# Token groups that follow the batches: one pooled attention and MLP kernel, regrouped

## The chip, the cores and the metric

The kernel runs on one core of one Trainium2 chip. The metric is device time in microseconds of one launch. The kernel before was run five times; one execution was also profiled, and every line of a profile below is from such an execution.

## What is computed

There are 8 batches of 8 heads with 576 queries of 64 numbers. Keys and values are averaged over runs of 8 positions, so that 72 of them stand against 576 queries. The attention output, with the heads side by side, gives 4608 tokens of 512 numbers, which pass a two-layer MLP with the activation h - tanh(h).

```python
def _attn_ref(q, k, v):
    k_p = k.reshape(B, H, Sp, pool, D).mean(axis=3)
    v_p = v.reshape(B, H, Sp, pool, D).mean(axis=3)
    scores = scale * np.matmul(q, k_p.transpose(0, 1, 3, 2))
    scores = scores - np.max(scores, axis=-1, keepdims=True)
    attn = np.exp(scores)
    attn = attn / (np.sum(attn, axis=-1, keepdims=True) + 1e-09)
    return np.matmul(attn, v_p).astype(np.float32)

def _moe_ref(x, w_in, w_out):
    h = x @ w_in
    g = h - np.tanh(h)
    return (g @ w_out).astype(np.float32)
```

## The kernel before

The MLP works on nine groups of 512 tokens (TG = 512, NG = 9). A batch has 576 tokens (S), so group g takes tokens 512g to 512g+511 across batch borders. Inside a batch the first 512 queries (QA) are held as position p*4 + j, so that a block of 128 tokens is one j; the last 64 (QT) are a tail block.

The order of all instructions is written out by hand, and each engine works through its own in that order. TensorE is PE in the profile, VectorE DVE, ScalarE ACT, GpSimd POOL; SP issues most of the DMAs.

**Groups 0 and 1.** Batch 0 is loaded, pooled and transposed on TensorE. Group 0's first layer runs tile by tile (`mlp_h`, L512), its second layer in 16 steps u (`mlp_o`, L540), with the preparation of batch 1 between them: `k_transpose`, `q_pe_transpose` (L217), `scores_wide`, `av` and `x_pe_transpose` (L475). The PSUM banks for all of these rotate over three.

**Groups 1 to 8.** A group has two stages.

- The h stage: 16 tiles of the first layer, four matmuls each (`h_mms`, L558), mostly in pairs. For a pair, ScalarE takes tanh (L570), VectorE subtracts (L571), and further VectorE operations form sums (P, Q). In this stage batch nb = g + 1 has its queries cast on ScalarE (`q_cast_part`, L192 and L197), and SP issues a transpose of k (L334) and five of q (L205). Then SP issues the loads of k, v and q of batch g + 2 (nine DMAs, about 3.4 MB), in one stream with the transposes. GpSimd finishes pooling, then issues the stores of group g - 1 (`store_tile`, L635) and places k (L302).
- The products: seven products of the second layer (a scheme that saves one of eight), each in two halves of eight matmul pairs, so u = 0 to 13 (L614), collected in two PSUM banks and combined by ScalarE and VectorE (`after_product`, L654 to L674). Between them stand the scores of batch nb (u = 0 to 4, each tile of 576 columns as two of 288, L351 and L370) and its attention blocks (u = 6, 7, 8, 9 and 11: `av_both`, matmuls L398, reciprocal L433, multiply L434). SP transposes each block of x into xT (L463) by DMA.

The activations for the MLP are in `xT`, a ring over three groups' tokens. Which blocks of a batch are transposed at once, and which wait for the next group's stage, follows from the group's border:

```python
            if b * S + blk * 128 < (b + 1) * TG:
                x_dma_transpose(b, blk, x_sb)
            else:
                late.append((b, blk, x_sb))
```

A block that crosses the end of the ring takes two transposes, and a tile of output that crosses a batch border takes two stores (`out_segments`).

**The end.** Group 8 has no attention beside it. Its last product is done token tile by token tile (L1025), each followed by a copy and its stores; the stores of the third and fourth output part go out from SP, GpSimd and ScalarE (L631, L1028). Line L1056 holds the program's closing waits.

Of the kernel before, what the change touches and what calls it, by code (L numbers as in the profile page):

```python
# [19 lines left out]
NHP = H // 2  # L20
# [3 lines left out]
T = B * S  # L24
NFB = DM // 128
# [9 lines left out]
RING = 3 * TG  # L35
# [7 lines left out]
def kernel(  # L43
# [54 lines left out]
    xT = const.tile([128, NFB, RING], BF16, name="xT")  # L98
# [100 lines left out]
    def q_dma_transpose(b, j0=0, j1=R + 1):  # L199
        if j0 == 0:  # L200
            qTs[b] = work.tile([128, NHP, S], BF16, name="qT", tag="qT")
        qT = qTs[b]
        for j in range(j0, j1):
            rows = 128 if j < R else QT
            nc.sync.dma_start_transpose(  # L205
                out=qT[:, :, j * 128 : j * 128 + rows],
                in_=q_bf[:rows, j, :, :].rearrange("p h d -> p (h d)"),
            )

    def q_pe_transpose(b, hps, eng=None):  # L210
        if b not in qTs:
            qTs[b] = work.tile([128, NHP, S], BF16, name="qT", tag="qT")
        qT = qTs[b]
        for hp in hps:
# [9 lines left out]
            evac(qT[:, hp, 0:QA], ps[:, :], eng)  # L224

    def q_pe_tail(b):
        ps = ps_any([128, NHP, QT], FP32, "qt_ps")
        for hp in range(NHP):
            nc.tensor.matmul(
                ps[:, hp, :],  # L230
                lhsT=q_bf[:, R, 2 * hp : 2 * hp + 2, :].rearrange("p h d -> p (h d)"),
                rhs=ident[:, 0:QT],
                start=True,
                stop=True,
            )
        evac(qTs[b][:, :, QA:S], ps[:, :, :])
# [109 lines left out]
    def score_mms(b, t, dst, c0, c1, pairs=range(NM)):  # L346
        for m in pairs if t == NM else (t,):
# [6 lines left out]
                rhs=qTs[b][:, m, c0:c1],  # L354
                start=True,
                stop=True,
            )

    def scores(b, t):
        if t == 0:  # L360
            E_tiles[b] = work.tile([128, NT, S], BF16, name="E", tag="E", bufs=1)
        E = E_tiles[b]
        hs = S // 2
        pss = []
        for half in range(2):
            ps = ps_b1([128, hs], FP32, "s_ps")
            score_mms(b, t, ps[:, :], half * hs, (half + 1) * hs)
            pss.append(ps)
        for half, ps in enumerate(pss):
            nc.scalar.activation(  # L370
                out=E[:, t, half * hs : (half + 1) * hs], in_=ps[:, :], func=ACT.Exp, scale=SCALE
            )

    def scores_wide(b, ts):
# [3 lines left out]
        for t in ts:  # L378
            ps = ps_any([128, QA], FP32, "s_ps")
            score_mms(b, t, ps[:, :], 0, QA)  # L380
            nc.scalar.activation(out=E[:, t, 0:QA], in_=ps[:, :], func=ACT.Exp, scale=SCALE)

    def scores_tail(b):
        ps = ps_any([128, NT, QT], FP32, "s_ps")
        for t in range(NT):
            score_mms(b, t, ps[:, t, :], QA, S)
# [36 lines left out]
    def new_x():  # L423
        return work.tile([128, 2, 4, D], BF16, name="x_sb", tag="x_sb", bufs=5)

# [15 lines left out]
    def av(b, blk, alloc, by_dma):  # L441
        x_sb = new_x()
        if by_dma:
# [4 lines left out]
        if by_dma:  # L448
            if b * S + blk * 128 < (b + 1) * TG:
                x_dma_transpose(b, blk, x_sb)  # L450
            else:
                late.append((b, blk, x_sb))
        return x_sb

    late = []

    def x_dma_transpose(b, blk, x_sb):
        p0 = 0 if blk < 4 else 64
        pos = (b * S + blk * 128) % RING
        p1 = min(128, p0 + RING - pos)  # L460
        for r0, r1, c in ((p0, p1, pos), (p1, 128, 0)):
            if r1 > r0:
                nc.sync.dma_start_transpose(  # L463
                    out=xT[:, :, c : c + r1 - r0],
                    in_=x_sb[r0:r1, :, :, :].rearrange("p a h d -> p (a h d)"),
                )

    def x_pe_transpose(b, blk, x_sb, fbs=(0, 4)):
        p0 = 0 if blk < 4 else 64
        pos = b * S + blk * 128  # L470
        f0, f1 = fbs
        xf = x_sb.rearrange("p a h d -> p (a h d)")
        ps = ps_any([128, f1 - f0, 128], FP32, "xT_ps")
        for fb in range(f0, f1):
            nc.tensor.matmul(  # L475
                ps[:, fb - f0, p0:128],
                lhsT=xf[:, fb * 128 : (fb + 1) * 128],
                rhs=ident[:, p0:128],
# [3 lines left out]
        nc.scalar.copy(out=xT[:, f0:f1, pos : pos + 128 - p0], in_=ps[:, :, p0:128])  # L482

    def out_segments(c0, nrows):
        segs = []
        r = 0
        while r < nrows:
            c = c0 + r
            bb = c // S
            i = c % S  # L490
            if i < QA:
                j = i // 128
                p0 = i % 128
                ln = min(128 - p0, nrows - r, QA - i)
                dst = out[bb * S : bb * S + QA, :].rearrange("(p j) m -> p j m", j=R)[
                    p0 : p0 + ln, j, :
                ]
            else:
                ln = min(S - i, nrows - r)
                dst = out[bb * S + i : bb * S + i + ln, :]  # L500
            segs.append((r, r + ln, dst))
            r += ln
        return segs
# [3 lines left out]
    def mlp_h_mms(g, i, f0, f1, pool=None):  # L507
        tok0 = g * TG
        if f0 == 0:
            h_tiles[i] = ps_h.tile([128, TG]) if pool is None else pool  # L510
        for fb in range(f0, f1):
# [3 lines left out]
                rhs=xT[:, fb, tok0 : tok0 + TG],  # L515
# [18 lines left out]
    def mlp_o(g, tb, i0, i1, gts, pool=None):  # L534
# [12 lines left out]
        if i1 == NHID:  # L547
# [4 lines left out]
            for r0, r1, dst in out_segments(g * TG + tb * 128, 128):  # L552
                nc.sync.dma_start(out=dst, in_=o_sb[r0:r1, :])

    def h_mms(g, i, dst):
        c0 = (g * TG) % RING
        for fb in range(NFB):
# [3 lines left out]
                rhs=xT[:, fb, c0 : c0 + TG],  # L561
# [66 lines left out]
    def store(g, th, engs, c0, c1):  # L628
        for tt in range(2):
# [431 lines left out]
```

## Time and profile before

| | us |
|---|---|
| median of 5 runs | 295.13 |
| lowest and highest | 293.11 and 297.32 |
| the profiled execution | 295.13 |
| its span, first to last instruction | 293.4 |
| TensorE busy | 279.9 |
| VectorE busy | 223.6 |
| ScalarE busy | 153.3 |
| GpSimd busy | 135.8 |
| h matmuls L558, 496 recorded | 112.6 |

DMA issues from the page:

| transfer | count | us from issue to landing, median |
|---|---|---|
| xT<-x_sb, transpose, SP | 32 | 3.4 |
| qT<-q_bf, transpose, SP | 30 | 2.5 |
| kT<-kd, transpose, SP | 6 | 3.1 |
| out<-O, 256 KB, GpSimd | 12 | 3.4 |
| out<-O, 128 KB, GpSimd | 32 | 3.6 |
| out<-O, 64 KB, SP | 12 | 2.2 |

How to read it: times are from the start of the span. A busy TensorE is not TensorE at its peak, since the ends of matmuls are modelled. "A <- B" in a list of waits means that A sat idle until B was done, with the total in us, the number of times and the longest. The time of a run is 1.7 us longer than the span.

### The profile page before, as it was taken

What the parts mean: (1) busy time and instruction counts of PE and PEld (TensorE: products, weight loads), DVE (VectorE), ACT (ScalarE), POOL (GpSimd) and SP (SyncE); (2) the same over time, 40 slices, a digit from 0 to 9 for tenths busy, and PEclk for the clock granted to TensorE, in tenths of its full rate; (3) what the DMA queues carried; (4) which work ended last, traced back from release to release, by engine and by line L of the source; (5) the groups of instructions that cost most, each with busy time, mean ns of one, the idle gap of its engine ahead of it and who ended that gap; (6) DMA issues with size and microseconds to landing.
All of it is one profiled execution on the core that took longest, in us unless ns stands there. A gap on an engine that the chain in (4) does not pass through costs nothing.

```text
span 293.4 us, 5359 instructions
## 1 busy us (share of the span) xinstructions
PE 279.9 (95%) x2017; PEld 179.0 (61%) x2036; DVE 223.6 (76%) x348; ACT 153.3 (52%) x242; POOL 135.8 (46%) x160
## 2 busy tenths in 40 slices
PE   7999989999999996999999999999999999999992
PEld 2454455446874685448954895489548944874681
DVE  5658665799977995389959967996799849927971
ACT  4737586586347732566176618661867046226510
POOL 8600818980299339900797089608960040030001
PEclk9999999999999999799999999999999999999998
DMA  7999999948835999599937996799581260021023
GB/s 253 229 213 282 308 210 315 303 90 303 193 78 109 287 303 115 123 243 324 84 76 186 351 188 87 196 343 182 78 205 28 56 171 2 0 77 69 0 57 89
DMA packets 65098, 49.91 MB, mean 170 GB/s; under 512 B 40336, under 2 KB 54032, under 8 KB 65072
## 3 DMA queue, kind: packets, MB, share of 16 engines
q1 hardware_dynamic: 55184, 35.53, 52.0%
q0 software_dynamic: 7312, 12.19, 18.3%
q10 hardware_dynamic: 2576, 1.84, 2.2%
q8 instruction: 16, 0.26, 0.4%
q14 instruction: 10, 0.08, 0.1%
HBM read 36.70 MB, written 9.44 MB: 157 GB/s over the span
## 4 chain that ended last, share of the span: by engine, by line
PE 84%; DVE 6%; DMA 3%; ACT 3%; issue 1%; SPq 0%; ACTq 0%; DVEq 0%
PE PS L558 34%; PE PS L614 33%; PE PS L540 5%; PE PS L398 4%; PE PS L351 4%; PE PS L512 2%; DMA k_raw<-in_k_dram 2%; DVE Gt L571 2%; DVE Gt L525 1%; DMA xT<-x_sb 1%; ACT q_bf L192 1%; DVE P L579 1%; ACT TS L570 0%; PE PS L475 0%; PE PS L800 0%
## 5 line engine op out<-in xcount | busy, mean ns | idle before, releaser
L558 PE MATMUL PS<-xT,w1b 128*128 128x512 bf16 x496 | 112.6, 383 | 3.1 <-DMA xT<-x_sb 2.3
L571 DVE TENSOR_TENSOR Gt<-PS,TS 128x1024 bf16<-128x1024 f32 x56 | 68.4, 1221 | 29.8 <-ACT TS L570 29.7
L558 PEld LDWEIGHTS <-w1b 128*128 128x128 f16 x512 | 50.3, 98 | 63.0 <-issue 5.0
L570 ACT ACTIVATE TS<-PS 128x1024 f32<-128x1024 f32 x56 | 57.4, 1025 | 34.4 <-PE PS L558 29.1
L248 POOL TENSOR_TENSOR k_raw<-k_raw 128x512 f32<-128x512 f32 (+2 forms) x13 | 21.1, 1639 | 75.9 <-DVE rden L433 46.2
L635 POOL DMA_DIRECT2D out_dram<-O x44 | 23.8, 547 | 39.9 <-DVE O L673 22.3
L614 PE MATMUL PS<-w2s,Dg 128*128 128x256 f16 x256 | 30.2, 273 | 0.0
L614 PEld LDWEIGHTS <-Gt 128*128 128x128 bf16 x256 | 24.4, 98 | 5.7 <-DVE Gt L576 0.5
L614 PEld LDWEIGHTS <-P 128*128 128x128 bf16 x256 | 24.6, 98 | 4.7 <-issue 1.4
L614 PEld LDWEIGHTS <-Dg 128*128 128x128 bf16 x256 | 24.5, 98 | 2.6
L434 DVE TENSOR_TENSOR x_sb<-PS,rden 128x512 bf16<-128x512 f32 x30 | 20.7, 691 | 6.8 <-DMA xT<-x_sb 5.9
L370 ACT ACTIVATE E<-PS 128x288 bf16<-128x288 f32 x60 | 21.4, 409 | 8.0 <-PE PS L351 7.6
L579 DVE TENSOR_TENSOR P<-Gt 128x1024 bf16<-128x1024 bf16 x32 | 22.2, 693 | 0.6
L398 PE MATMUL PS<-VB,E 128*128 128x130 bf16 x240 | 20.2, 220 | 0.1
L670 ACT COPY m<-PS 128x512 f32<-128x512 f32 x8 | 4.7, 586 | 29.5 <-PE PS L614 29.5
L269 POOL TENSOR_TENSOR v_raw<-v_raw 128x512 f32<-128x512 f32 (+1 forms) x12 | 20.1, 1694 | 0.0
L589 DVE TENSOR_TENSOR Dg<-Gt 128x1024 bf16<-128x1024 bf16 x32 | 19.9, 683 | 0.0
L398 PEld LDWEIGHTS <-E 128*128 128x128 bf16 x240 | 16.8, 98 | 1.9 <-issue 0.4
L351 PE MATMUL PS<-qT,KB 128*128 128x288 bf16 (+5 forms) x128 | 17.0, 289 | 0.2
L614 PE MATMUL PS<-w2s,Gt 128*128 128x256 f16 x128 | 16.7, 273 | 0.3 <-DVE Gt L576 0.2
L1021 ACT COPY O<-PS 128x512 f32<-128x512 f32 x7 | 4.1, 586 | 24.5 <-PE PS L614 24.5
L614 PE MATMUL PS<-w2s,P 128*128 128x256 f16 x128 | 16.3, 273 | 0.0
(112 smaller groups left out, 387.5 us busy)
## 6 DMA issues: line engine op xcount, KB each, us to landing
k_raw<-in_k_dram SPq DMA_DIRECT2D x7, 1024.0 KB, 8.7
q_raw<-in_q_dram SPq DMA_DIRECT2D x7, 1024.0 KB, 11.8
v_raw<-in_v_dram SPq DMA_DIRECT2D x7, 1024.0 KB, 11.9
out_dram<-O POOLq DMA_DIRECT2D x32, 128.0 KB, 3.6
out_dram<-O POOLq DMA_DIRECT2D x12, 256.0 KB, 3.4
w1b<-in_moe_w_in_dram POOLq DMA_DIRECT2D x4, 512.0 KB, 13.9
w2b<-in_moe_w_out_dram POOLq DMA_DIRECT2D x4, 512.0 KB, 17.1
out_dram<-O SPq DMA_DIRECT2D x4, 256.0 KB, 4.5
```

Source lines behind the costliest of these rows:

```text
L248: first = eng.tensor_tensor(out=r[:, ta:tb, 0:4, :], in0=r[:, ta:tb, 0:4, :], in1=r[:, ta:tb, 4:8, :], op=ALU.add)
L269: eng.tensor_tensor(out=r[:, ta:tb, 0:4, :], in0=r[:, ta:tb, 0:4, :], in1=r[:, ta:tb, 4:8, :], op=ALU.add)
L351: nc.tensor.matmul(dst[p : p + w], lhsT=KB[b % 2][:, o : o + w], rhs=qTs[b][:, m, c0:c1], start=True, stop=True,)
L370: nc.scalar.activation(out=E[:, t, half * hs : (half + 1) * hs], in_=ps[:, :], func=ACT.Exp, scale=SCALE)
L398: nc.tensor.matmul(ps[:, 2 * n : 2 * n + 2, :].rearrange("p h d -> p (h d)") if n < 2 else ps.rearrange("p (a s) d -> p a s d", s=2)[:, :, ...
L434: nc.vector.tensor_tensor(out=x_sb[:, :, :, :], in0=ps[:, :, :, 0:D], in1=rden[:, :, :, :].to_broadcast([128, 2, 4, D]), op=ALU.mult,)
L558: nc.tensor.matmul(dst, lhsT=w1b[:, fb, i * 128 : (i + 1) * 128], rhs=xT[:, fb, c0 : c0 + TG], start=(fb == 0), stop=(fb == NFB - 1),)
L570: nc.scalar.activation(out=t2, in_=PS[:, b0 : b0 + 2, :], func=ACT.Tanh)
L571: nc.vector.tensor_sub(out=Gt[:, p, :, :], in0=PS[:, b0 : b0 + 2, :], in1=t2)
L579: nc.vector.tensor_tensor(out=P[:, a:b, :], in0=Gt[:, a:b, 0, :], in1=Gt[:, a:b, 1, :], op=ALU.add)
L614: nc.tensor.matmul(part(g, bk, tt), lhsT=lhs(k, slice(tt * 128, (tt + 1) * 128)), rhs=rhs[:, k, :], start=(first and k == 0 and (tt == 0 o ...
L635: nc.gpsimd.dma_start(out=dst, in_=O[r0:r1, tb, :])
```

## The change

Groups 0 to 7 now are the first 512 queries of batches 0 to 7, and group 8 is the eight tails of 64. So `xT` becomes two tiles used in turn, each [128, 4 blocks, 4 feature blocks, 128], and a third, `xT_last`, for group 8. A group's right-hand operand for L558 comes from four pieces of 128 columns. All four blocks of batch g + 1 are due at the start of group g + 1.

The blocks of x are kept in pairs, and one DMA transposes a pair, 128 x 1024; the tail block has its own. Queries do the same: two transposes of 1024 columns and one of the tail, for five of 512. In groups 1 to 6, scores are formed as 512 columns per tile (`scores_wide`) at u = 0 to 4 and the tails of all tiles at u = 5 (`scores_tail`); the attention blocks come at u = 5, 6, 7, 8 and 10. Batch 0's tail goes to xT_last by DMA, not through TensorE; the tail of batch 1 is transposed at the start of group 1. One q transpose of batch 1 on TensorE moves from u = 3 to u = 4, and the next two one step on.

A group's stores on GpSimd are two of 512 KB. In group 8 each store is two, by partition halves (the two batches of a token tile), on SP or on SP and ScalarE, none on GpSimd; both last copies are VectorE's.

```diff
-    xT = const.tile([128, NFB, RING], BF16, name="xT")
+    xT = [const.tile([128, 4, NFB, 128], BF16, name=f"xT{i}") for i in range(2)]
+    xT_last = const.tile([128, 4, NFB, 128], BF16, name="xT_last")
...
+    def q_dma_transpose(b, n):
+        qT, qt = q_tiles(b)
+        if n < 2:
             nc.sync.dma_start_transpose(
-                out=qT[:, :, j * 128 : j * 128 + rows],
-                in_=q_bf[:rows, j, :, :].rearrange("p h d -> p (h d)"),
+                out=qT[:, 2 * n : 2 * n + 2, :, :].rearrange("p j h c -> p (j h) c"),
+                in_=q_bf[:, 2 * n : 2 * n + 2, :, :].rearrange("p j h d -> p (j h d)"),
+            )
...
+    def x_dma_transpose(b, n):
+        if n < 2:
+            nc.sync.dma_start_transpose(
+                out=xT[b % 2][:, 2 * n : 2 * n + 2, :, :].rearrange("p k f c -> p (k f) c"),
+                in_=x_pairs.pop((b, n)).rearrange("p k a h d -> p (k a h d)"),
+            )
+        else:
+            c = (b % 2) * QT
+            nc.sync.dma_start_transpose(
+                out=xT_last[:, b // 2, :, c : c + QT],
+                in_=x_pairs.pop((b, 2))[128 - QT : 128].rearrange("p a h d -> p (a h d)"),
+            )
...
     def h_mms(g, i, dst):
-        c0 = (g * TG) % RING
+        x = xT[g % 2] if g < NB else xT_last
...
-                rhs=xT[:, fb, c0 : c0 + TG],
+                rhs=x[:, :, fb, :],
...
+    def store(g, t0, t1, eng, c0=0, c1=DM):
+        if g < NB:
+            eng.dma_start(out=out_part(g, t0, t1, c0, c1), in_=O[:, t0:t1, c0:c1])
+        else:
+            for k, dst in enumerate(out_part(g, t0, t1, c0, c1)):
+                eng[k].dma_start(out=dst, in_=O[k * QT : (k + 1) * QT, t0:t1, c0:c1])
...
         if i == 11:
-            x4 = av(0, 4, ps_any, False)
-        if i == 13:
-            x_pe_transpose(0, 4, x4)
+            av(0, 4, ps_any, False)
+            x_dma_transpose(0, 2)
...
-            q_pe_transpose(1, (0, 1), "act")
+            q_pe_transpose(1, (0,), "act")
         if u == 4:
-            q_pe_transpose(1, (2,), "act")
+            q_pe_transpose(1, (1,), "act")
...
-        if u == 5:
-            q_pe_transpose(1, (3,), "act")
+        if u in (5, 6):
+            q_pe_transpose(1, (u - 3,), "act")
...
+            if g == 1 and p == 0:
+                x_dma_transpose(1, 2)
             if g > 1 and p == 0:
-                for tb in (2, 3, 0, 1):
-                    store_tile(g - 1, tb)
+                store(g - 1, 2, 4, nc.gpsimd)
+                store(g - 1, 0, 2, nc.gpsimd)
...
-                q_dma_transpose(nb, 2 * c, min(2 * c + 2, R + 1))
+                q_dma_transpose(nb, c)
...
-        while late:
-            x_dma_transpose(*late.pop(0))
...
-                    scores(nb, u)
+                    scores_wide(nb, (u,))
                 if u == NT:
-                    ps_a.n += 2
-                if u in (6, 7, 8, 9, 11):
-                    av(nb, (6, 7, 8, 9, 11).index(u), ps_b1, True)
+                    scores_tail(nb)
+                if u in (5, 6, 7, 8, 10):
+                    blk = (5, 6, 7, 8, 10).index(u)
+                    av(nb, blk, ps_b1, True)
+                    if blk in (1, 3, 4):
+                        x_dma_transpose(nb, blk // 2)
...
-    store(NG - 1, 1, (nc.sync, nc.gpsimd), HD, DM)
+    ends = (nc.sync, nc.scalar)
+    store(NG - 1, 2, 4, ends, HD, DM)
     bk, lhs, rhs = products[6]
-    for tt, eng in ((0, nc.scalar.copy), (1, nc.vector.tensor_copy)):
+    for tt in range(2):
         product(NG - 1, bk, lhs, rhs, 0, NP, False, (tt,))
-        eng(out=O[:, tt, 0:HD], in_=part(NG - 1, C1, tt))
-        for n, (r0, r1, dst) in enumerate(out_segments((NG - 1) * TG + tt * 128, 128)):
-            (nc.scalar if n else nc.sync).dma_start(
-                out=dst[:, 0:HD], in_=O[r0:r1, tt, 0:HD]
-            )
+        nc.vector.tensor_copy(out=O[:, tt, 0:HD], in_=part(NG - 1, C1, tt))
+        store(NG - 1, tt, tt + 1, ends, 0, HD)
```

## The prediction, made before the result was known

> **What bounds the kernel now.** I read the page first: the busy shares, the granted clock and the chain that ended last.
>
> ```profile
> span 293.4 us, 5359 instructions
> PE 279.9 (95%) x2017; PEld 179.0 (61%) x2036; DVE 223.6 (76%) x348; ACT 153.3 (52%) x242; POOL 135.8 (46%) x160
> PEclk9999999999999999799999999999999999999998
> PE 84%; DVE 6%; DMA 3%; ACT 3%; issue 1%; SPq 0%; ACTq 0%; DVEq 0%
> ```
>
> TensorE is the bound nearly everywhere. The change neither adds nor removes matmul columns in groups 1 to 8, so what is at stake is the idle time of TensorE: who is late where. One slice has a lower clock. Next, the busy time in windows laid on groups 2 to 6 (h matmuls, then products):
>
> ```profile
> core 0: us, PE busy (x) PEld busy (x) DVE busy (x) ACT busy (x) POOL busy (x), PEclk, DMA share, GB/s
> 85.40:117.10 31.70, 29.31 (x221) 19.70 (x223) 24.85 (x37) 17.76 (x28) 21.91 (x25) 1.00 0.91 194
> 117.10:148.00 30.90, 30.79 (x221) 20.21 (x223) 23.68 (x34) 14.95 (x25) 14.78 (x17) 0.94 0.85 184
> 148.00:177.20 29.20, 29.09 (x221) 19.67 (x223) 22.36 (x32) 16.32 (x27) 18.60 (x21) 1.00 0.87 203
> 206.50:235.70 29.20, 29.09 (x221) 19.77 (x223) 24.76 (x38) 16.32 (x27) 11.55 (x17) 1.00 0.51 98
> ```
>
> A full group costs 29.2 us; group 2 costs 2.5 more and group 3 costs 1.7 more at a clock of 0.94. The chain in order of time, between them and one group later, and the list of waits:
>
> ```profile
> 112.83 0.56 PE PS L614 x6
> 113.39 3.33 DMA xT<-x_sb
> 116.86 0.38 PE PS L558
> 117.29 12.42 PE PS L558 x49
> ...
> 148.19 10.74 PE PS L558 x49
> ```
>
> ```profile
> DVE x_sb L434 <- DMA xT<-x_sb: 5.9, 3, 2.3
> PE PS L558 <- DMA xT<-x_sb: 2.3, 1, 2.3
> ```
>
> Group 3's first matmul waited 2.3 us for a transpose that landed late behind the loads of k, v and q, and the same 49 matmuls then took 12.42 instead of 10.74 us. One late transpose cost 2.3 + 1.7 = 4.0 us. At the other boundaries TensorE went straight on. That is the resource which the change moves.
>
> **What the Trainium skill says.** "TensorE: Matmul & The Clock Gate", Part 1: after an idle window of about 3.4 us the clock halves, and a busy window restores it. The trace agrees: 1.7 us lost is half of about 3.4 us, after an idle of 2.3. "DMA: Bandwidth & Descriptors", Rules for kernel authors: merge small transfers, and two transfers by partition halves don't run faster than one. The trace fits: the 64 KB stores at the end land after 2.2 to 2.4 us whatever the queue. No page prices the wide transpose.
>
> **Part 1: what a group waits for.** Before, group g needed of the newest batch only the blocks below token (g+1)*512: blocks 0 to 2 for batches 2 and 3, two for 4 and 5, one for 6 and 7. After, it needs all four, in two transposes of 1024 columns. The price of a wide one is not in the trace; nearest are these, both on an empty queue (first kT, 640 columns; then xT, 512):
>
> ```profile
> DMA to landing us min/median/max: 2.6/2.6/2.6
> DMA to landing us min/median/max: 2.4/2.4/2.4
> ```
>
> To the hundredth, 2.58 and 2.42: 0.16 for 128 columns. SP's issue is 1.20 against 1.19, so nearly fixed. A wide one: 2.42 + 4 x 0.16 = 3.06 us. Bounds: 2.4 (width free) to 4.9 (as two narrow ones in sequence). I take 3.06, because kT has the same form of operands.
>
> When is the second one issued? It waits for VectorE, so I replay group 6, which has no loads:
>
> ```profile
> 227.51 0.69 DVE L661 TENSOR_TENSOR m<-O,m 128x512 f32<-128x512 f32 x1
> ...
> 228.36 0.69 DVE L434 TENSOR_TENSOR x_sb<-PS,rden 128x512 bf16<-128x512 f32 x1
> ...
> 228.99 0.69 DVE L665 TENSOR_TENSOR O<-m,PS 128x512 f32<-128x512 f32 x1
> ...
> 235.42 2.32 PE L558 MATMUL PS<-xT,w1b 128*128 128x512 bf16 x9
> ```
>
> Attention moves one half product earlier (u = 5, 6, 7, 8), but VectorE reaches block 0 only after L661, so at 228.0 (0.1 sooner, as three scores before it are 0.03 shorter). A block is reciprocal plus multiply, 0.87 from start to start; L665 takes 0.61. So 228.0 + 2 x 0.87 + 0.61 + 2 x 0.87 = 232.1: block 3 is ready before m451 (L671), behind which it stood until now. First wide issue at 229.9, second at 232.2, landing 235.3, and TensorE follows a landing by 0.11. It wants xT at 235.42: stall about 0, no margin. Behind SP's wait for block 3 stand only the tail's transpose and the next kT, which GpSimd's kd holds anyway; behind L558's wait stands all of TensorE.
>
> Groups 3 to 5 have the same VectorE offsets (first multiply 8.35 us after the first product matmul in groups 2, 5 and 6), but loads in the ring. These ended 12.4 us into the products in groups 4 and 5. Three q transposes instead of five (SP was at them 6.4 us) let SP issue the loads about 1.9 us earlier; the stores on GpSimd, same 1 MB in two DMAs for six to eight, begin at the same time. Where both met the last q transpose, the transfer rate fell to about 100 to 210 GB/s for 2.5 us; I count 1.5 us earlier, 10.9. The first wide one then drains after them, and the second, issued at 12.2, isn't held. I charge 0.1 each for groups 3 to 6: 0.4.
>
> Group 2: loads ended 14.4 us into the products; 2 us earlier is 12.4. Two wide transposes queue behind, 1.5 us of packets each (kT: 640 packets in 0.93 us), plus 0.45 to land: 15.85 against 15.4. Stall 0.5; no clock loss. So of the 4.0 us, 3.5 come back.
>
> Group 1: VectorE has two w_sum pieces of 0.68 more. Block 0 is done at 79.86, block 1 at 80.7, L665 at 81.3, blocks 2 and 3 at 82.2 and 83.1; landing 83.15 + 3.06 = 86.2, plus 0.11. TensorE began group 2 at 85.19. Stall 1.1 (bounds 0.4 to 3.0).
>
> The VectorE waits of 5.9 us on x_sb go too (pairs with two buffers, so a batch never meets its own transposes), but were off the path, as were ScalarE's exps: ten of 0.409 become five of 0.597 and one of 0.432, 0.7 less per batch. Score columns stay the same. The moving operand now comes in four pieces of 128; L800 reads in pieces of 64 and takes 274 ns where whole 256-column operands take 273: nothing.
>
> **Part 2: groups 0 and 1.** The four L475 matmuls of batch 0's tail go; TensorE stood about 0.6 us there around 32.3. But next it needs kd of batch 1, which GpSimd finishes at 37.62, and it was there at 37.8: 0.15 survives. Then q's second transpose moves one step later:
>
> ```profile
> 39.22 0.38 PE L217 MATMUL PS<-ident,q_bf 128*128 128x128 bf16 x4 [0.74 <-DVE KB L303]
> ```
>
> This wait for a PSUM bank (0.74) is filled by four output matmuls. The first score then waits for ScalarE's copy at 39.66, which eats the 0.15. Net gain 0.75 (bounds 0 and 0.9). Group 1's start passes it on: q of batch 2 lands at 57.2, the cast would want it at 57.3. Batch 0's and 1's tail transposes on SP come before its load of k (held to 41.9 by w2) and before the first q transpose (held by its cast): nothing.
>
> **Part 3: the end.** All instructions of the last line, by engine:
>
> ```profile
> L1056 POOLq DRAIN  x3: 46/93/5206, 287.4 to 293.1; - x3
> L1056 SPq DRAIN  x3: 7/7/13, 291.0 to 292.9; - x3
> ```
>
> GpSimd's drain runs from 287.43 to 292.64, while SP has seen the last store by 291.0. It stands behind two stores issued from GpSimd at 287.0. Without them it can start at about 263, and the end is SP's. There, SP's last issue moves from 288.59 to about 288.23 (one store per half and tile on each of SP and ScalarE), ScalarE's stays at 288.23 and lands at 290.55. SP is through by 290.9; the closing handshake took 0.74: 291.6 against 293.4, gain 1.8 (bounds 0, were the drain a fixed cost, and 2.1). VectorE takes both last copies: the first fits between 286.9 and 287.3.
>
> **The sum.** 293.4 - 0.75 - 4.0 + (1.1 + 0.5 + 0.4) - 1.8 = 288.85 us span. Around the span the profiled execution had 295.13 - 293.4 = 1.7, giving 290.6 us. Its own time is also the median of the five runs, so no shift: 1.5% faster. Differences under 1% can't be told from none here.
>
> **Rivals.**
> A, chance 0.15: at 2 to 3, the loads hold the last transposes as long as now, and the clock drops again. For it: DMA engines are 0.91 busy in that stretch. Against it: they start two microseconds earlier. Adds 2.3 + 1.7 - 0.5 = 3.5: 294.1, within 1%.
> B, chance 0.12, the slower side: the wide transpose costs what two cost, 4.9. Then groups 3 to 6 stall 1.8 each, group 1 2.9 and group 2 2.3, sum 12.4, and the last two pay the clock, 3.4. 293.4 - 6.55 + 15.8 + 1.7 = 304.4. It decides from 3.9 us on: six boundaries times 0.83 and the 1.6 of groups 1 and 2 are the 6.55 gained. For it: all six boundaries have no margin, where the kernel before had 0.1 to 1.4 us in groups 3 to 5. Against it: kT's slope.
> C, chance 0.07: GpSimd's drain and the start give nothing: 290.6 + 2.55 = 293.2, within 1%.
> Forecast, chance 0.66, own range 288.4 to 292.2: 288.55 is the same sum with no stalls, less 0.15 if the start brings its bound of 0.9. The upper end is drawn to 294.5 to take in A and C; B is left out. Faster 0.68, within 1% 0.20, slower 0.12.
>
> **What would show it.** Right: wide transposes landing in about 3.1 us on an empty queue; group 1 to 2 a wait of about 1 us of L558 on xT; group 3's h matmuls at full clock; no long GpSimd drain at the end and the span ending about 1.1 us after the last landing; the 0.74 us wait at L217 gone. Wrong: waits of L558 on xT at every boundary, or several low clock slices.

## The result, and the profile after

The changed kernel takes 292.31 us (median of 43 runs, 291.22 to 294.73). The kernel before takes 293.38 us in the runs beside it (80 runs, 291.24 to 297.85). The ratio is 0.9973 with a 95% interval of [0.9961, 0.9984]: faster by 0.3%, where 1.5% was forecast. It leaves out the runs more than 1.5% above the fastest of their kernel, so it is not the quotient of the two medians. A later pairing on another chip gave 0.9952 [0.993, 0.9974]. Experiment 1 finds 0.2% between two sets of runs of one program, so a gain of 0.3 to 0.5%, found in two pairings, is hardly larger than that. The median lies in the stated range only because its upper end was drawn up for rivals A and C; the forecast's own range ended at 292.2, and its case, faster by over 1%, did not come.

The page of the changed kernel, the lines that answer to those of before:

```profile
span 290.4 us, 5231 instructions
PE 280.7 (97%) x2031; PEld 177.8 (61%) x2032; DVE 220.4 (76%) x349; ACT 151.1 (52%) x216; POOL 117.8 (41%) x128
PEclk9999999999999999999999999999999999999999
PE 72%; DMA 13%; DVE 6%; POOL 4%; ACT 1%; issue 1%; SPq 1%; POOLq 0%; DVEq 0%; ACTq 0%
```

The span is 3.0 us shorter, the clock is full throughout, and TensorE's recorded busy time is 0.8 us longer although it has no more columns to do. That last figure is the one to stop at, as a hint and not a measure: 2017 matmuls were recorded before and 2031 after. Windows on groups 2, 3 and 6, each from its first h matmul to that of the next group:

```profile
core 0: us, PE busy (x) PEld busy (x) DVE busy (x) ACT busy (x) POOL busy (x), PEclk, DMA share, GB/s
86.60:116.05 29.45, 29.44 (x222) 19.58 (x223) 23.03 (x34) 15.49 (x21) 15.71 (x16) 1.00 0.76 204
116.05:145.50 29.45, 29.45 (x224) 19.66 (x223) 23.05 (x34) 16.10 (x22) 15.51 (x16) 1.00 0.78 203
204.40:233.85 29.45, 29.45 (x225) 19.67 (x223) 22.93 (x34) 16.10 (x22) 8.82 (x12) 1.00 0.40 83
```

The groups are now alike, with no idle time in them, but an undisturbed group takes 29.44 us where it took 29.22. By the stages (from first matmul to first matmul) the h stage is 13.81 in both kernels and the product stage 15.63 for 15.41. The only wait at a boundary is group 1 to 2, in the chain in order of time:

```profile
82.73 0.67 DVE x_sb L424
83.41 0.05 issue
83.45 3.02 DMA xT<-x_sb
86.47 0.14 issue
86.61 3.40 PE PS L534 x15
```

VectorE's multiply of block 3, the second wide transpose, TensorE 0.14 behind its landing. The list of waits gives 0.7 us for it, against 1.1 forecast. The wide transposes of group 6, with an empty queue, and at the end the closing drains:

```profile
L452 SPq DMA_TRANSPOSE xT<-x_sb x2: 1232/1232/1233, 228.0 to 230.3; - x2
DMA to landing us min/median/max: 3.0/3.0/3.0
```

```profile
L1032 SPq DRAIN  x3: 7/7/13, 289.6 to 289.9; - x3
L1032 POOLq DRAIN  x2: 46/74/102, 289.9 to 290.2; - x2
```

A wide transpose lands after 3.05 us (to the hundredth, in the trace) where 3.06 was worked out, and is issued 12.09 us into the products where 12.2 was. GpSimd's drain of 5.2 us is gone.

So most single steps came out as they were put down, yet the sum did not. The experiments ask three things: what the kernel before loses ordinarily, why a product stage is 0.22 longer, and where the gain of the start went. The last ones try to make a faster kernel of the answers.

### The profile page after: what moved, and what is told of

Same layout as the page of the kernel before. It is cut to its first block, busy times and chain, and to the rows that moved or that the text cites. A ratio compares the mean times of both kernels' runs of the same rounds, so it can differ in the third digit from the quotient of the medians.

```text
span 290.4 us, 5231 instructions
## 1 busy us (share of the span) xinstructions
PE 280.7 (97%) x2031; PEld 177.8 (61%) x2032; DVE 220.4 (76%) x349; ACT 151.1 (52%) x216; POOL 117.8 (41%) x128
## 4 chain that ended last, share of the span: by engine, by line
PE 72%; DMA 13%; DVE 6%; POOL 4%; ACT 1%; issue 1%; SPq 1%; POOLq 0%; DVEq 0%; ACTq 0%
PE PS L534 33%; PE PS L590 30%; DMA w1b<-in_moe_w_in_dram 4%; DMA k_raw<-in_k_dram 4%; DMA q_raw<-in_q_dram 4%; PE PS L391 3%; PE PS L359 3%; DVE Gt L547 2%; PE PS L517 2%; DMA xT<-x_sb 1%; POOL k_raw L256 1%; DVE w2s L573 1%; DVE x_sb L424 1%; ACT TS L546 1%; DVE Dg L565 1%
## 5 line engine op out<-in xcount | busy, mean ns | idle before, releaser
L534 PE MATMUL PS<-xT,w1b 128*128 128x512 bf16 x448 | 98.0, 379 | 1.2 <-DMA xT<-x_sb 0.7
L546 ACT ACTIVATE TS<-PS 128x1024 f32<-128x1024 f32 x56 | 57.4, 1024 | 31.0 <-PE PS L534 26.8
L374 ACT ACTIVATE E<-PS 128x512 bf16<-128x512 f32 x40 | 23.7, 598 | 12.1 <-PE PS L359 12.0
L606 POOL DMA_DIRECT2D out_dram<-O x14 | 7.8, 559 | 46.4 <-DVE O L647 44.2
L277 POOL TENSOR_TENSOR v_raw<-v_raw 128x512 f32<-128x512 f32 (+1 forms) x12 | 19.2, 1618 | 0.0
L424 DVE TENSOR_TENSOR x_sb<-PS,rden 128x512 bf16<-128x512 f32 x24 | 16.6, 691 | 0.8
L590 PE MATMUL PS<-w2b,Gt 128*128 128x256 f16 x128 | 16.3, 273 | 0.0
L590 PE MATMUL PS<-w2s,Q 128*128 128x256 f16 x128 | 16.3, 273 | 0.0
```

The costliest lines, as they stand in the source:

```text
L277: eng.tensor_tensor(out=r[:, ta:tb, 0:4, :], in0=r[:, ta:tb, 0:4, :], in1=r[:, ta:tb, 4:8, :], op=ALU.add)
L424: nc.vector.tensor_tensor(out=x_sb[:, :, :, :], in0=ps[:, :, :, 0:D], in1=rden[:, :, :, :].to_broadcast([128, 2, 4, D]), op=ALU.mult,)
L534: nc.tensor.matmul(dst, lhsT=w1b[:, fb, i * 128 : (i + 1) * 128], rhs=x[:, :, fb, :], start=(fb == 0), stop=(fb == NFB - 1),)
L546: nc.scalar.activation(out=t2, in_=PS[:, b0 : b0 + 2, :], func=ACT.Tanh)
L590: nc.tensor.matmul(part(g, bk, tt), lhsT=lhs(k, slice(tt * 128, (tt + 1) * 128)), rhs=rhs[:, k, :], start=(first and k == 0 and (tt == 0 o ...
```

## The experiments

Spans are of the profiled execution, ratios are against the kernel before on the same chip. "Product stage" is always from the first product matmul to the next group's first h matmul. In the views, a q behind an engine's name marks its instruction stream, where it waits or issues DMAs, and PEld is TensorE's loading of weights.

**1. The kernel before, again.** No edit.

> The kernel before, unchanged. Theory: the execution that the prediction was worked out from was a dear one; an ordinary execution waits less for xT at the start of group 3, and mostly without the clock drop of 1.7 us. Then the new profile shows TensorE waiting 0 to 2.3 us there, group 3's first 49 matmuls in about 10.7 us, a granted clock of 0.995 or more and a span near 291.7. Rival: the 4.0 us belong to every execution, and the later runs are shorter for another reason spread over the span; then the profile again shows a wait of about 2.3 us, 12.4 us for those matmuls and a clock near 0.991.

Measured: 293.42 us, ratio 1.0023 [1.0004, 1.0043], span 291.2. One program against itself: differences of 0.2% mean nothing, whatever the interval says. The chain of work at the boundary of groups 2 and 3:

```profile
111.25 1.55 PE PS L614 x15
112.79 3.43 DMA xT<-x_sb
116.22 0.14 issue
116.35 2.75 PE PS L558 x12
```

The same late transpose, but TensorE stood 1.3 us and not 2.3, and the h stage after it took 13.81 us: no loss of clock. Group 2's product stage was 16.83, so the loss is 1.4 us (16.83 - 15.41). In the next experiment, which leaves this part alone, it was 1.7. The 4.0 us in the prediction were those of one dear execution.

How rare such an execution is, the other runs tell, since each lists its granted clock. The profiled one had 0.991. Of 174 runs of the kernel before on four chips, 23 had 0.988 to 0.992, and these took 295.05 to 297.92 us (two more had a clock under 0.8 and took far longer). So by its clock about one run in seven or eight is of this kind. Of 66 listed runs of the changed kernel none was under 0.996: the change does take this loss away, but a median holds little of it.

**2. The end alone.** The kernel before, one store moved from GpSimd to ScalarE:

```diff
-    store(NG - 1, 1, (nc.sync, nc.gpsimd), HD, DM)
+    store(NG - 1, 1, (nc.sync, nc.scalar), HD, DM)
```

> The kernel before with one word changed: the second store of group 8's last store call goes out from ScalarE, not GpSimd. Theory: GpSimd's closing drain stands behind its own last stores, so the drain of 5.2 us goes, and the program ends about 0.8 us after the last landing: 1.4 to 1.8 us less, ratio 0.994 to 0.995. Rival: the drain has a fixed cost, or the end is set by the landing of the last store anyway: ratio 1.000.

Measured: 292.51 us, 0.998 [0.9953, 1.0006], span 290.3. From group 8's first product matmul to the end of the span it is 17.26 us, against 18.11 in both executions of the kernel before: 0.85 of the 1.39 that the whole change brings there (16.72). ScalarE's timeline shows where most of the rest went:

```profile
284.51 1.40 ACTq L631 DMA_DIRECT2D out_dram<-O  x2
286.01 0.37 ACT L1026 COPY O<-PS 128x256 f32<-128x256 f32 x1 [3.38 <-DVE O L1026]
286.41 1.38 ACTq L1028 DMA_DIRECT2D out_dram<-O  x2
```

Its copy, of the first of the last two tiles, stood behind its own two issues of 0.7 us each, so its last store went out late. The bracket names VectorE's copy of the other tile, which ended at the same time. But in the kernel before, with no issues ahead of it, the copy came 11.6 us into the products, and here at 12.9. The change gives both last copies to VectorE, which issues nothing. So the two edits seem to belong together; the second was not run alone.

**3. Batch 0's tail transposed later.** The changed kernel, its tail transpose moved from 33 us to group 1 (and two buffers for the tail block):

```diff
             av(0, 4, ps_any, False)
-            x_dma_transpose(0, 2)
...
             if g == 1 and p == 0:
+                x_dma_transpose(0, 2)
                 x_dma_transpose(1, 2)
```

> The changed kernel with batch 0's tail transposed at the start of group 1, beside batch 1's, and not at 33 us. Theory: that transpose, in the queue among the loads of w2, v and k, makes the third w2 load land 2 us later (43.9 against 41.9), and with it the loads of batch 2, whose q then holds up ScalarE at 58.4; without it the w2 load lands near 42 and group 1's products begin 0.8 to 1.2 us sooner (68.3 to 68.6 against 69.4), ratio to the changed kernel about 0.997. Rival: the w2 load is late by chance or for its own later issue; then it still lands at 43 to 44 and nothing is gained.

Measured: 291.48 us, 0.9945 [0.9931, 0.996], span 289.7. SP in the changed kernel, and in this one:

```profile
32.99 1.28 SPq L458 DMA_TRANSPOSE xT_last<-x_end  x1
43.95 0.39 SPq L138 DMA_DIRECT2D k_raw<-in_k_dram  x1
```

```profile
41.71 0.37 SPq L138 DMA_DIRECT2D k_raw<-in_k_dram  x1
```

The load of k waits for the third load of the second weight, and it goes out 2.2 us earlier without the transpose in front; group 1's products start at 68.66 instead of 69.42. Over all runs here it starts at 41.7 to 42.1 us in the four kernels with the late tail, at 42.0 to 42.3 in three executions of the kernel before (which transposes this tail on TensorE), and at 42.8 to 44.6 in seven with the tail at 33 us. One DMA transpose of 64 rows in the middle of the weight load puts the next load back by some 0.5 to 3 us. That is shown; how the two get in each other's way inside the queues is not. Where TensorE then pays differs: in the changed kernel ScalarE stood 0.57 us for q of batch 2 in group 1's h stage, in its second execution (experiment 9) TensorE stood 0.5 us for the weight itself.

**4. The tail's scores twice.** The eight matmuls of 64 columns are issued a second time into the same bank, each tile's directly behind its first, so that they stay one visit:

> The changed kernel with the eight matmuls of a score tail issued twice in groups 1 to 6 (same values written again). Theory: these short matmuls cost their weight loads, not their columns: 0.26 us for a tail, so 1.6 us more in all, and a group of 29.7 us for 29.44. Rival, the prediction's reckoning by columns: five times 64 columns at 2.4 columns per ns are 0.13 us, so 0.8 us more in all and 29.57 for a group.

Measured: 292.8 us, 1.0002 [0.9983, 1.0021]. Product stage 15.77, 0.14 more than 15.63, what the prediction's reckoning by columns gives (0.13); the theory of weight loads is out. The set takes 0.35 us where it stands, so 0.21 of that is paid on entering it and not for each small matmul. TensorE's timeline shows what that is, in the kernel before (group 4) and after (group 2):

```profile
166.04 1.04 PE L614 MATMUL PS<-w2s,P 128*128 128x256 f16 x8
167.01 0.43 PE L351 MATMUL PS<-qT,KB 128*32 128x288 bf16 x8
167.37 1.05 PE L614 MATMUL PS<-w2s,P 128*128 128x256 f16 x8
168.26 1.04 PE L614 MATMUL PS<-w2b,Gt 128*128 128x256 f16 x8
```

```profile
104.78 1.04 PE L590 MATMUL PS<-w2s,P 128*128 128x256 f16 x8
105.74 0.40 PE L359 MATMUL PS<-qT,KB 128*32 128x512 bf16 x4
106.08 1.05 PE L590 MATMUL PS<-w2s,P 128*128 128x256 f16 x8
106.96 0.42 PE L359 MATMUL PS<-qt,KB 128*128 128x64 bf16 x8
107.31 0.52 PE L391 MATMUL PS<-VB,E 128*128 128x130 bf16 x6
```

The fifth key tile is computed with four weights of 32 columns (128*32). From 166.04 to 167.01 is 0.97, where eight such product matmuls otherwise go in 0.87 to 0.89, and the set itself takes 0.36 where another tile's scores, of as many columns, take 0.25. Before, all 576 query columns met the 32-column weights in one visit; after, 512 in one and 64 in another, hidden in the form "128x64 x8", of which four are 128*32. The Trainium skill says it, "TensorEngine Tiling (Array Packing)", Key Properties: changing the tiling mode drains TensorE. The trace fits, with 0.1 us lost ahead of the set and 0.1 within it. The runs give the price here, 0.2 us for each visit; that the drain is what is paid is the skill's word, as no run separates it.

**5. One visit instead of two.** Each tile's tail goes directly behind its 512 columns:

```diff
+        score_mms(b, t, ps[:, :], False)
+        score_mms(b, t, tails[b][:, t, :], True)
...
-                    scores_tail(nb)
+                    exp_tail(nb)
```

> The changed kernel with each tile's score tail issued right behind the same tile's 512 columns in groups 1 to 6, so that the 32-column matmuls of tile 4 and of its tail stand together; the exp of the tails stays at u = 5. Theory: a set of 32-column matmuls has a fixed price of about 0.22 us, whatever its columns; the changed kernel pays it twice per group, the kernel before once; together they pay it once: products of 15.41 us for 15.63, 1.3 us less over six groups. Rival: the price is that of short matmuls as such (weight loads that nothing hides): then 15.6 or more, as five short ones now stand apart.

Measured: 292.49 us, 0.9964 [0.9944, 0.9984], span 291.0. The product stage is 15.41 again where it isn't disturbed: the price is shown by its removal too. But the time isn't better than the changed kernel's. At the boundary of groups 2 and 3:

```profile
112.89 4.14 DMA xT<-x_sb
117.03 0.14 issue
117.17 1.46 PE PS L553 x6
```

The second wide transpose landed after 4.14 us and not 3.05, and TensorE waited 0.9 us; 0.35 more in group 5, and 0.8 at group 2. Of the 0.9, 0.2 is the shorter stage itself: in the changed kernel TensorE took this landing up without a wait, but with nothing to spare. The rest is the landing. In this transpose's time, and in that of the changed kernel's at the same place (3.43), the trace has an 8 KB transfer of instructions on one of the DMA engines that carry it. That goes beyond one boundary. Ten executions of kernels with paired transposes are on record (all but experiment 8), with 120 wide transposes. In the time of 53 of them no instruction transfer ran, and all of these landed after 3.02 to 3.10 us. In the time of 67 one ran, and 43 of these landed later, up to 4.87. In experiment 4, with more matmuls in each group, one transfer of 16 KB moved: it falls 2.8 us behind the first wide issue in group 4 and not in group 3, and the late landing goes with it (4.80 in group 4 and 3.08 in group 3; in the changed kernel 3.07 and 4.85). So the two belong together; no experiment was made to move such a transfer alone.

**6. Group 1's weight sum on GpSimd.** Two VectorE operations stand among group 1's products and push block 3 back; they are moved to GpSimd.

> The changed kernel with the two weight sums of group 1's products (0.68 us each on VectorE) moved to GpSimd, behind its placing of k. Theory: they delay block 3 of batch 2 and are all of the wait at the start of group 2; it falls from 0.66 to 0, and group 1's products from 17.18 to about 16.5. Rival: GpSimd's sums run beside VectorE in a stage that VectorE bounds and slow it by as much, or the wait is set by the landing of the wide transpose: nothing is gained.

Measured: 293.69 us, 1.0034 [1.0011, 1.0056]. The wait at group 2 is gone, but VectorE's sums beside GpSimd's (66 to 71 us) tell of a new one. Groups of that stretch, this kernel and then the changed one:

```profile
L555 DVE TENSOR_TENSOR P<-Gt 128x1024 bf16<-128x1024 bf16 x3 | 3.8, 1281 | 0.0
L547 DVE TENSOR_TENSOR Gt<-PS,TS 128x1024 bf16<-128x1024 f32 x3 | 3.6, 1210 | 0.0
```

```profile
L547 DVE TENSOR_TENSOR Gt<-PS,TS 128x1024 bf16<-128x1024 f32 x3 | 3.6, 1213 | 0.0
L555 DVE TENSOR_TENSOR P<-Gt 128x1024 bf16<-128x1024 bf16 x3 | 2.1, 697 | 0.0
```

The sums with both operands in SBUF take 1.28 us on average instead of 0.70; the subtractions, with one operand in PSUM, are unmoved at 1.21. TensorE waited 1.9 us at 71.1. The Trainium skill has the rule, "SBUF — State Buffer", Who interferes with whom: a VectorE instruction with two SBUF inputs contends with a GpSimd instruction that reads SBUF, and one with at most one SBUF input, outside the 2-port modes, does not. The trace agrees in both halves, by 1.28 for 0.70 us and by the unmoved 1.21.

**7. Queries in narrow transposes.** q's two wide transposes as four, so SP issues its loads later.

> The changed kernel with q's two wide transposes as four narrow ones. Theory, the prediction's: SP gets to the loads about 2 us later, they end about 12 us into the products for 10.2, and the wide transposes of x queue behind them: waits for xT of 0.3 to 0.6 us at the starts of groups 3 to 6, 1 to 2 us in all, a granted clock still above 0.99. Rival: VectorE alone sets when the second transpose of x goes out, and the loads have room: no waits there, the same time as the changed kernel within 0.3 us.

Measured: 292.02 us, 0.9958 [0.9941, 0.9976], span 290.4, no wait at any boundary but group 2's. The loads ended 10.95 us into group 2's products, where they end at 10.1 in the changed kernel and at 12.84 in the kernel before (experiment 1). So a third of their advance was given back, and it cost nothing. In the changed kernel's second execution (experiment 9) they ended at 11.44, with no wait there either. The earlier loads, which the prediction made the reason for the gain at 2 to 3, show no worth between 10.1 and 11.4; the rest of the way, to 12.8 and beyond, wasn't tried.

**8. x in narrow transposes.** The opposite half: one transpose for each block of x.

```diff
-                    if blk in (1, 3, 4):
-                        x_dma_transpose(nb, blk // 2)
+                    x_dma_transpose(nb, blk // 2, blk)
```

> The changed kernel with one transpose for each block of x, so four narrow ones for two wide. Theory: the last block is all that counts; it goes out at the same time and lands in 2.4 us for 3.05, so the wait at the start of group 2 falls by 0.6 and elsewhere nothing changes: 0.3 to 0.7 us less than the changed kernel. Rival: four issues of 1.2 us on SP in a row, at blocks that come 0.87 us apart, put the last one back by 0.6 us or more: the same time or up to 1 us longer.

Measured: 295.31 us, 1.0088 [1.0056, 1.0119], span 293.5, with waits of 0.7 to 0.9 us in four groups. SP in group 3's products, and the chain at their end; then SP in the changed kernel:

```profile
140.36 6.21 SPq L452 DMA_TRANSPOSE xT<-x_sb  x4
146.66 1.20 SPq L458 DMA_TRANSPOSE xT_last<-x_end  x1
```

```profile
145.35 2.45 DMA xT<-x_sb
```

```profile
139.73 4.23 SPq L452 DMA_TRANSPOSE xT<-x_sb  x2
144.20 1.17 SPq L458 DMA_TRANSPOSE xT_last<-x_end  x1
```

A transpose keeps SP for about 1.2 us whether it is wide or narrow. VectorE was done with block 3 at 143.41, but three issues stood ahead of it, the third held for 2.27 us, and its own went out at 145.35. In the changed kernel the second wide one went out at 141.96, 0.02 after block 3 was done. But the row of issues is not the whole of it. The chain at the end of group 2's products, where TensorE waited 0.8 us:

```profile
113.92 3.49 DMA xT<-x_sb
117.41 0.14 issue
```

Here the last transpose went out 13.0 us into the products, 0.9 later than the second wide one does, and with the usual 2.44 us it would have landed in time, with 0.1 to spare. It landed after 3.49, and the one in group 5 after 3.39. In the time of both the trace has an 8 KB transfer of instructions, and in that of the long issue in group 3 one of 16 KB, as in experiment 5. By these figures two wide transposes leave 0.4 us of room for such a delay (12.08 + 3.05 + 0.14 of 15.63), and four narrow ones 0.1. The delay itself is not one of SP's issues.

**9 to 11. Putting it together.** First the changed kernel again on that chip, then with the late tail of experiment 3 and group 1's weight sum on VectorE in its idle time at 44.5 us, then with two more edits: experiment 5's order of scores, and one of VectorE's four differences behind block 3.

```diff
         if u == 8:
             scores_tail(1)
+            w_sum(w2s[:, 2, :, :], b21, b22, ALU.add)
...
-                if g == 1 and n in (1, 2):
-                    w_sum(w2s[:, 2, :, :], b21, b22, ALU.add, k0=4 * n - 4, k1=4 * n)
```

> The changed kernel unchanged, beside the two that follow on one chip. Expected: span 290.4, a wait of about 0.7 us at the start of group 2, product stages of 15.63 us, third load of the second weight at 43.9 us, and about 0.997 of the kernel before. If the lost start is a matter of one profiled execution and not of the kernel, the third weight load lands at 42 here and group 1's products start at 68.7 instead of 69.4.

> The changed kernel with two edits: batch 0's tail transpose behind the key transpose of group 1, and group 1's weight sum (the third summed weight of the products) made on VectorE in its idle stretch of 44.7 to 46.5 us of group 0 instead of between group 1's products. Theory (the first product stage waits at its end because VectorE reaches the last two blocks of attention late, by its weight sums): the wait of 0.66 us at the start of group 2 goes, and with the 0.75 us of the start the span is 289.0, time about 0.992 of before. Rival (the wait stands on the row of transposes on SP, not on VectorE): the wait stays, span 289.7, 0.9945 as with the first edit alone. Second rival: 1.24 us of VectorE at 44.7 us push group 0's attention back and TensorE waits there by 0.3 us or more.

> The two edits of the run before it, and two more: the score columns of the tail behind each tile's 512 columns (one set of 32-column matmuls for each group instead of two), and the last of the four differences of VectorE moved behind the attention of block 3, so that block 3's multiply, and its transpose, come about 0.7 us earlier. Theory (0.22 us for each of six product stages, and the waits of 0.9 and 0.35 us that the first of these brought when it stood alone were the margin that the shorter stage used up, given back by the earlier transpose): product stages 15.41, no wait over 0.2 us at any stage's start, span about 287.7, 0.988 of before. Rival (the transposes' landing is set by what else is on the DMA queues, not by VectorE): product stages 15.41, but waits of 0.4 to 0.9 us in two or three groups, span 289.0 to 289.5, no better than the two edits alone.

Measured: 292.12 us, 0.9952 [0.993, 0.9974], for the changed kernel (span 290.8, wait 0.7, product stage 15.63 as before; k's load at 44.6, group 1's products from 69.8: the lost start is the kernel's own). 291.35 us, 0.9934 [0.991, 0.9958], for the two edits (span 289.6). 295.32 us, 1.007 [1.0045, 1.0096], for the four (span 293.4).

With two, the wait at group 2 went as the theory had it, and 0.75 us came back in group 1's h stage, which nobody had foretold: 15.0 us for 14.25 in experiment 3. VectorE there, in experiment 3 and then here:

```profile
55.22 1.33 DVE L573 TENSOR_TENSOR w2b<-w2b 128x2048 f16<-128x2048 f16 x1
58.59 1.15 DVE L573 TENSOR_TENSOR w2s<-w2b 128x512 f16<-128x512 f16 x1
```

```profile
55.26 2.10 DVE L573 TENSOR_TENSOR w2b<-w2b 128x2048 f16<-128x2048 f16 x1
58.64 1.91 DVE L573 TENSOR_TENSOR w2s<-w2b 128x512 f16<-128x512 f16 x1
```

The early sum had held up GpSimd's own (5.40 us for four, 4.49 without it), GpSimd's later pooling moved back by 0.8 us, and VectorE's next sums met it at another phase. That this phase is the cause is argued from the order; experiment 12 takes the sums out of the stage and doesn't test the phase.

With four, both theories were wrong. VectorE in group 2's products:

```profile
112.83 1.47 DVE L584 TENSOR_TENSOR Dg<-Gt 128x1024 bf16<-128x1024 bf16 x1
114.21 2.02 DVE L666 TENSOR_TENSOR m<-m,m 128x512 f32<-128x512 f32 x1
116.39 0.69 DVE L443 TENSOR_TENSOR x_end<-PS,rden 128x512 bf16<-128x512 f32 x1
```

The moved difference takes 1.47 us for 0.68, and the subtraction behind it, also of two SBUF operands, 2.02 for 0.82 in the changed kernel: GpSimd's pooling of the next batch runs from 109.1. Both kernels hold that pooling back by an explicit dependence (`gate`, on the last of VectorE's early SBUF subtractions); I had moved a difference past the gate. TensorE waits 0.2 to 0.5 us for the difference and 0.4 for the tail block's bank, and the product stage is 16.38 in groups 2 to 5. In group 6, where GpSimd has nothing to pool, it is 15.41 with no wait.

**12. No weight sums in group 1 at all.** As the two edits, and group 1's other weight sum also early:

```diff
             scores_tail(1)
+            w_sum(w2s[:, 2, :, :], b21, b22, ALU.add)
+            w_sum(w2s[:, 0, :, :], b11, b22, ALU.add, k0=0, k1=4)
...
+                else:
+                    w_sum(w2s[:, 0, :, :], b11, b22, ALU.add, k0=4, k1=NP)
...
-            if g == 1 and p < 4:
-                w_sum(w2s[:, 0, :, :], b11, b22, ALU.add, k0=2 * p, k1=2 * p + 2)
```

> The changed kernel with batch 0's tail transpose behind group 1's key transpose, the weight sum of group 1's products made on VectorE at 44.5 us of group 0, and now also the four pieces of the other weight sum, which VectorE made between group 1's subtractions (3.3 us there): half of it at 45.7 us, half at 53.4 us. Theory (group 1's hidden layer is VectorE's: in the run with the two edits, GpSimd's sums took 5.40 us instead of 4.49 beside VectorE's early one, its later work moved back by 0.8 us, VectorE's first two sums in group 1 took 2.10 and 1.91 us instead of 1.33 and 1.15, and the stage 15.0 us instead of 14.25): without sums between them the subtractions take the stage at TensorE's pace, 13.8 to 14.1 us, span 288.5 to 288.8, 0.989 to 0.990 of before. Rival (what VectorE takes early it takes from GpSimd, whose keys and values of batch 2 then come too late): the wait moves to group 1's first score matmuls at 68 to 70 us, and the span is 289.6 or above, 0.9934.

Measured: 290.49 us, 0.9893 [0.9845, 0.994], span 288.7: the theory's numbers, and the fastest kernel here. Group 1's h stage, with the two edits and then with this one:

```profile
54.45:69.45 15.00, 14.13 (x65) 6.26 (x64) 14.62 (x15) 9.32 (x10) 11.17 (x11) 1.00 0.82 211
55.40:69.20 13.80, 13.80 (x65) 6.27 (x64) 12.30 (x13) 9.70 (x11) 11.71 (x11) 1.00 0.76 183
```

With VectorE busy for 14.62 of 15.00 us the stage was VectorE's; with 12.30 of 13.80 it is TensorE's. Not all is gain: the early sums take 2.78 us beside GpSimd's, group 0's attention starts 1.1 us later, and group 1 begins at 55.4 instead of 54.45. The clean h stage gives 1.2, and the product stage, without its wait, is 15.70 against 16.37 with the two edits.

## Why the prediction was wrong, point by point

The dear profiled execution, which the first point below is about, is left out of this table: it sets the changed kernel against the second execution of the kernel before (experiment 1), on the spans. The forecast for the boundary 2 to 3 is written with that execution's own loss.

| step | forecast, us | found, us |
|---|---|---|
| start, to group 1's products | -0.75 | -0.1 (69.42 against 69.49) |
| group 1's products | +1.1 | +1.0 (17.18 against 16.21) |
| group 2's products, ordinary loss 1.4 | -0.9 | -1.2 (15.65 against 16.83) |
| groups 3 to 6 | +0.4 | +0.9 (4 x 0.22) |
| end | -1.8 | -1.4 (16.72 against 18.11) |
| sum | -1.95 | -0.8 (290.4 against 291.2) |

The table is kind to the start. Three executions of the kernel before, experiment 2's among them, begin group 1's products at 69.03, 69.32 and 69.49, two of the changed kernel at 69.42 and 69.84. The forecast was made from the one with 69.03. So the start gave nothing, or cost some tenths.

1. **The base was the step that failed most.** "Its own time is also the median of the five runs, so no shift." The five runs' median was 295.13; over 80 runs it is 293.38. The profiled execution had a 2.3 us wait and a loss of clock of 1.7 at one boundary; two other executions show 1.4 and 1.7 in all. So about 2.4 of the 4.0 us that the change was to save are there in about one run of seven or eight. The spans fell short of the forecast by 3.75 us (0.8 for 4.55), and this step is 2.6 of it. The line of waits and the clock row were read correctly; that they were typical was assumed, and the range of the runs (293.11 to 297.32) was not held against it. "The trace agrees", of the clock, holds for the 1.7 us only: the idle stretch before it, 2.3 us, is shorter than the window of about 3.4 that the prediction names, and waits of 1.3 and 1.5 us at the same place cost no clock. Why this one did stays open.

2. **"Score columns stay the same: nothing."** It was 0.22 us in each of six groups, 1.3 in all. The columns are the same, the number of visits to the 32-column tiling mode is doubled. Experiments 4 and 5 show the price by adding and removing, and the trace of before already had it: the 0.97 ahead of the set and its 0.36. The allowance of 0.1 for each of groups 3 to 6 was for late landings. Some came, up to 3.32 us for the second wide one, but the stage hid them.

3. **"Batch 0's and 1's tail transposes on SP: nothing."** Batch 0's fell into the weight load, which the next loads wait for, and cost the 0.75 forecast there: L217's wait of 0.74 us for a PSUM bank did go, but SP's loads of k started 0.5 to 3 us later. Moving this one transpose brought 0.76 us back (69.42 to 68.66, experiment 3). The prediction counted SP's queue and not what shares the DMA engines at 33 us.

4. **The end, 1.8: the mechanism held, the size was 1.4.** The last store landed at 289.09, 2.5 us after VectorE's last copy, and the span ended 1.35 behind it. SP's closing waits go in a fixed order, and in the trace the one for this last landing came first, so that eight more followed it (0.5 us). The forecast had counted 1.1 from landing to end. (Not all 64 KB stores before landed after 2.2 to 2.4 us: one of ScalarE's two took 2.85. And no run compares a store with its two halves.)

5. **Boundary 2 to 3: the right outcome, with its reason open.** Full clock, as said; a stall of 0.5 was forecast, none came. Two things changed there: the loads ended 1.4 to 2.8 us earlier than in experiment 1, and two transposes go out for five. Which of them does it isn't shown. Experiment 7 gives back too little of the first, and experiment 8, with four issues, is mixed with late landings. In three executions of the kernel before, the loads of group 2 ended at 12.85, 13.12 and 14.48 us into the products, and the last transpose went out at 13.3, 13.5 and 14.4. That fits the prediction's reason; in the changed kernel it goes out at 12.1, when VectorE is done. The price of the wide transpose, its issue time and group 1's wait were worked out from two neighbouring rows and from a replay of VectorE's order, and these held to within 0.1, 0.1 and 0.4 us. Group 1's shorter wait is in part the second point again: its products lasted 0.22 longer.

6. **The rivals.** None of the three came in its own form, though the range was drawn up for A and C and the median needed that room: this was luck. (Their chances add to 0.22, where 0.20 stands for within 1%.) A (the backlog holds the transposes) and B (4.9 us for a wide one) are out by the waits and by the 3.05 us. C had "the start gives nothing" right, but not the end, and put it down to no cause.

## What to carry to other kernels

Before a saving is priced from one profile, ask whether the loss in it is there every time: a stall with a second loss behind it (here the clock) makes a profiled execution dear. A second profile of the same kernel, or the granted clock of its other runs, costs less than a wrong base. Equal columns aren't equal time on TensorE: count how often a stretch enters another tile shape, not only what it does there. And where VectorE and GpSimd both work from SBUF, moving an operation between them, or past a gate that keeps them apart, shifts who meets whom; move it to where the other engine rests, and look at the stage that follows too.

## What the runs showed of the hardware that I had not expected

- Entering a set of 128*32 matmuls costs TensorE 0.2 us, however few follow (experiments 4 and 5).
- A DMA transpose of 64 rows at 33 us delays the end of a running weight load, and so the next loads, by some 0.5 to 3 us (experiment 3).
- Wide transposes land after 3.02 to 3.10 us when no transfer of instructions runs in their time; every later landing, up to 4.87, has one (120 of them in ten executions, experiment 5).
- VectorE's sums with two SBUF operands are slowed by GpSimd from 0.70 to 1.28 us on average, and a single subtraction to 2.0 for 0.8; operations with a PSUM operand aren't (experiments 6 and 11).
- One kernel against itself, 22 and 67 runs on one chip, gave 1.0023 with an interval that excludes 1 (experiment 1).
